# A 64-point transform folded into even and odd halves, inside a long convolution kernel

## The chip, the cores and the metric

The kernel runs on one core of a Trainium2 chip. The metric is the device time of one execution in microseconds. Besides the five engines the text speaks of their queues: SP issues most transfers, ACT some of the first ones. PE is the matrix engine, PEld its weight loads, DVE the vector engine, ACT the scalar engine, POOL GpSimd.

## What is computed

Eight sequences of 3200 positions with 256 channels go through a filter in the frequency domain and then through a gated convolution:

```python
def _attn_ref(x, w_r, w_i, b_r, b_i):
    X = np.fft.rfft(x, axis=1)
    Yr = Xr @ w_r - Xi @ w_i + b_r
    Yi = Xr @ w_i + Xi @ w_r + b_i
    Yr = np.sign(Yr) * np.maximum(np.abs(Yr) - lam, 0.0)   # lam = 0.01
    Yi = np.sign(Yi) * np.maximum(np.abs(Yi) - lam, 0.0)
    return np.fft.irfft(Y, n=x.shape[1], axis=1)
def _moe_ref(x, w_val, conv_w, w_out):
    # gate = sigmoid of a causal 5-tap convolution over positions, per channel
    return (gate * (x @ w_val)) @ w_out
```

The output of the first is the input of the second. Everything is float32, and products that must keep that precision are done either as float32 (two instructions for each product in the trace) or as three float32r products of a high and a low part.

## The kernel before

The 3200-point transform is split as 64 x 50: a position is n2 x 64 + n1 with n1 of 64 (`N1`) and n2 of 50 (`N2`). The first stage (`p1`, and `p1_first` for batch 0) is a 50-point transform over n2: each load brings four n1 for all n2 and all channels of each of two halves of n1, products with the constant `f1` of 50x50 run in quarters of the 128x128 array (50x64 weights, 512 columns), ACT copies both banks of 512 to a tile `s`, and the tile is stored to a scratch tensor `a_dram` in DRAM. In it, frequency t (25 of them, each with a real and an imaginary row, 128 rows of n1 in all) comes first, so that it can be read back (tile `a`) with the 128 rows on the partitions.

The second stage (`s2` in `p2`) is the 64-point transform over n1 with twiddle factors folded into its constant `f2`: for each t and each half of the channels one product with 128x128 weights (the data) and 128 columns (the constant, real and imaginary part). A unit u is two t, and a batch has 13 units, the last of which holds only the 25th t. Its result in PSUM (`ps_s2`, two buffers) is copied and split: ACT copies the imaginary half (L651) and casts all to its high part (L655); DVE adds real and imaginary (L658) and forms the low part (L659); ACT and DVE do the same with the sum (L662, L663). Then `mix_sum` (L676) and `mix` (L671) multiply with the filter weights in three products instead of four, DVE seeds the accumulators with the bias (L680), ACT and DVE apply the soft threshold (L687, L689). The inverse 64-point transform `s1i` (L712) works on two units in 64x64 quarters, with its constant `g1`; ACT copies the result (L723), and it is stored to `z_dram`.

After a whole batch has been stored, `positions` reads it back and does the inverse 50-point transform (`s2i`, L771, 50-column quarters), and `gated` does the value product, the convolution (ACT for the first tap, DVE for four more, L833), the sigmoid, the gate product (L845) and the output product, eight blocks per batch.

`g1` is not loaded: in batch 0 `make_g1` transposes each unit of `f2` on PE with an identity matrix `eye` (L428), and ACT scales it into place (L430).

The order on each engine is fixed when the program is built. Every step is a piece given to `Plan.add` with a due time `at` (in units; a batch is 13, and the stages of neighbouring batches overlap by the offsets in `O`), an engine, an estimated length, what it uses and what it sets. `Plan.order` lists the pieces of each engine by simulating them: among the pieces that can begin soonest it takes the one with the lowest due time. Pieces of PE have a mode, "q" for quarters, "f" or "r" for full size; a change between them costs in that model, and `together` and `hold` favour quarters next to quarters. A PSUM or SBUF buffer is reused in a ring whose size is in `SLOTS`; four tiles of two banks are shared out as two `ps_2` pairs (first stage, s1i, s2i, value and output product) and the single-bank tags.

Batch 0 starts with its own scheme: x is loaded from two queues (SP and ACT), units are done in pairs, one half evicted by DVE and the other by ACT (L523), and stores follow on both queues. Loads of constants wait for marks such as `STORED` (all first-stage stores of batch 0 issued).

## Time and profile before

| | |
|---|---|
| three runs, us | 882.78, 884.87, 886.38 (median 884.87) |
| the profiled execution, us | 881.84 (span of its instructions 880.0) |
| granted PE clock over the span | 0.99 |
| HBM traffic in the span | read 82.04 MB, written 78.64 MB |

The costliest groups on PE and DVE, in the page's fifth part: line, engine, operation, tile written and read, shapes and count, then busy time in us and the mean of one in ns, then the idle time of the engine just before them and what ended it.

```profile
L833 DVE SCALAR_TENSOR_TENSOR acc<-y_sb,cw_sb,acc 128x400 f32<-128x400 f32 x512 | 298.9, 626 | 1.7 <-ACT acc L830 1.2
L671 PE MATMUL y_ps<-w_sb,xs 128*128 128x256 f32 x1152 | 156.9, 285 | 0.6 <-DVE y_ps L680 0.3
L600 PE MATMUL s<-f_sb,a 128*128 128x128 f32 x800 | 111.6, 282 | 4.7 <-DMA f_sb<-in_f 2.9
```

Matmuls are pipelined, so the mean of one is longer than the distance to the next. Buffer numbers are left out of names: `s` is any of the tiles s1, s2; `f_sb` and `g_sb` are the constants of the two transforms; `y_p` is the result of the inverse 50-point transform.

### The profile page before, as it was taken

How to read it: one execution, taken by the hardware profiler on the slowest of the kernel's cores; microseconds unless marked ns; L12 is line 12 of the kernel's file. 1: busy time of each engine (PE TensorE's matmuls, PEld its weight loads, DVE VectorE, ACT ScalarE, POOL GpSimd, SP SyncE). 2: the span in 40 equal slices, each digit the busy share in tenths (PEclk: the TensorE clock that was granted, in tenths of full speed). 3: DMA queues.
4: the chain of work that ended last, by engine and by line, in shares of the span. 5: the costliest groups of instructions: out<-in, count | busy, mean ns of one | idle time of the engine just before them, and what ended most of it. 6: DMA issues, size and time to landing. Idle time of an engine off the chain costs nothing.

```text
span 880.0 us, 24764 instructions
## 1 busy us (share of the span) xinstructions
PE 857.8 (97%) x10358; PEld 736.3 (84%) x10358; DVE 733.8 (83%) x1289; ACT 620.3 (70%) x1046; POOL 3.7 (0%) x11
## 2 busy tenths in 40 slices
PE   6989999999999999999999999999999999999997
PEld 2468778999888999889888998889989899998774
DVE  0345778999988988798889988888997999999896
ACT  1256667878778777787787777787777876776674
POOL 0000000000000000000000000000001000000000
PEclk8889999999999999999999999999999999999999
DMA  7788887743775467654765557654665535423622
GB/s 173 213 220 250 212 255 230 250 145 127 228 243 180 144 207 227 226 168 149 232 216 181 171 178 242 219 168 155 213 211 188 163 116 185 129 93 116 203 75 75
DMA packets 103955, 162.29 MB, mean 184 GB/s; under 512 B 9666, under 2 KB 78148, under 8 KB 103844
## 3 DMA queue, kind: packets, MB, share of 16 engines
q1 hardware_dynamic: 102756, 157.44, 56.3%
q10 hardware_dynamic: 1088, 3.28, 1.5%
q8 instruction: 81, 1.33, 0.6%
q14 instruction: 30, 0.25, 0.1%
HBM read 82.04 MB, written 78.64 MB: 183 GB/s over the span
## 4 chain that ended last, share of the span: by engine, by line
PE 87%; DVE 5%; DMA 5%; ACT 1%; issue 1%; SPq 0%; ACTq 0%
PE y_ps L671 16%; PE o_ps L803 14%; PE v_ps L803 13%; PE s L600 10%; PE z_ps L712 9%; PE k_ps L676 8%; PE y_p L771 7%; PE p L553 6%; DVE acc L833 3%; DMA x<-in_x 2%; PE v_ps L799 2%; DMA a_dram<-s 1%; DMA f_sb<-in_f 1%; PE y_ps L636 1%; PE turned L428 1%
## 5 line engine op out<-in xcount | busy, mean ns | idle before, releaser
L833 DVE SCALAR_TENSOR_TENSOR acc<-y_sb,cw_sb,acc 128x400 f32<-128x400 f32 x512 | 298.9, 626 | 1.7 <-ACT acc L830 1.2
L671 PEld LDWEIGHTS y_ps<-w_sb,xs 128*128 128x128 f32 x1152 | 143.2, 188 | 18.2 <-DVE acc L833 8.5
L671 PE MATMUL y_ps<-w_sb,xs 128*128 128x256 f32 x1152 | 156.9, 285 | 0.6 <-DVE y_ps L680 0.3
L803 PE MATMUL o_ps<-gated,wo_sb 128*128 128x400 f32 x744 | 149.5, 348 | 0.0
L803 PEld LDWEIGHTS o_ps<-gated,wo_sb 128*128 128x128 f32 x744 | 134.7, 188 | 2.5
L803 PE MATMUL v_ps<-y_hl,wv_sb 128*128 128x400 f32 x648 | 129.4, 346 | 0.0
L600 PEld LDWEIGHTS s<-f_sb,a 128*128 128x128 f32 x800 | 101.4, 194 | 18.5 <-issue 9.8
L600 PE MATMUL s<-f_sb,a 128*128 128x128 f32 x800 | 111.6, 282 | 4.7 <-DMA f_sb<-in_f 2.9
L803 PEld LDWEIGHTS v_ps<-y_hl,wv_sb 128*128 128x128 f32 x648 | 114.4, 188 | 0.4 <-ACT acc L830 0.4
L689 DVE SCALAR_TENSOR_TENSOR tp<-y_ps,tp 128x512 f32<-128x512 f32 (+1 forms) x104 | 69.1, 664 | 52.1 <-ACT tp L687 51.3
L687 ACT ACTIVATE tp<-y_ps,nlam 128x512 f32<-128x512 f32 (+1 forms) x104 | 69.7, 670 | 39.5 <-PE y_ps L671 23.2
L318 ACT CAST gated<-acc 128x800 fp32r<-128x800 f32 x62 | 53.5, 862 | 62.1 <-DVE acc L845 60.3
L712 PE MATMUL z_ps<-tp,g_sb 64*64 64x256 f32 x1536 | 92.8, 379 | 0.0
L676 PE MATMUL k_ps<-w_sb,xs 128*128 128x256 f32 x576 | 85.7, 283 | 0.2 <-DVE y_ps L680 0.2
L843 ACT ACTIVATE acc<-acc 128x400 f32<-128x400 f32 x128 | 66.9, 538 | 22.4 <-DVE acc L833 22.1
L676 PEld LDWEIGHTS k_ps<-w_sb,xs 128*128 128x128 f32 x576 | 75.4, 188 | 4.0 <-issue 1.8
L771 PEld LDWEIGHTS y_p<-g_sb,zl 50*64 50x64 f32 x4096 | 67.2, 135 | 13.4 <-issue 3.7
L712 PEld LDWEIGHTS z_ps<-tp,g_sb 64*64 64x64 f32 x1536 | 55.2, 133 | 27.3 <-issue 4.9
L830 ACT ACTIVATE acc<-y_sb,cw_sb 128x400 f32<-128x400 f32 x128 | 76.3, 630 | 1.7 <-DVE gated L320 1.6
L771 PE MATMUL y_p<-g_sb,zl 50*64 50x50 f32 x4096 | 71.5, 219 | 2.5 <-DVE acc L845 1.9
L680 DVE TENSOR_TENSOR y_ps<-k_ps,bias_sb 128x512 f32<-128x512 f32 x96 | 66.4, 692 | 1.8 <-PE k_ps L676 0.5
L659 DVE TENSOR_TENSOR xs<-s,xs 128x512 fp32r<-128x512 f32 x96 | 65.2, 680 | 1.2 <-ACT xs L655 1.1
(79 smaller groups left out, 953.4 us busy)
## 6 DMA issues: line engine op xcount, KB each, us to landing
zl<-z_dram SPq DMA_DIRECT2D x128, 200.0 KB
out<-o SPq DMA_DIRECT2D x63, 400.0 KB
a<-a_dram SPq DMA_DIRECT2D x96, 256.0 KB
z_dram<-z_t SPq DMA_DIRECT2D x48, 512.0 KB
x<-in_x SPq DMA_DIRECT2D x96, 200.0 KB
a_dram<-s SPq DMA_DIRECT2D x96, 200.0 KB
x<-in_x SPq DMA_DIRECT2D x24, 192.0 KB
a_dram<-s SPq DMA_DIRECT2D x24, 192.0 KB
```

What stands on the lines that cost most here:

```text
L600: nc.tensor.matmul(spec()[:, c, :, i, :], tl[ka][:, i, c * P:(c + 1) * P], f2_of(i), start=True, stop=True)
L671: nc.tensor.matmul(p[:, 1 - r, :], xm(hx, c, r), w_sb[:, m, hw, c, :], start=False, stop=k == 5, skip_group_check=True)
L676: nc.tensor.matmul(p, sm(hx, c), w_sb[:, 0, hw, c, :], start=k == 0, stop=k == 5)
L680: nc.vector.tensor_tensor(out=buffer(ky, "ps_y", [P, 2, D]), in0=tl[kk].rearrange("p (a d) -> p a d", a=1).to_broadcast([P, 2, D]), in1=bi ...
L687: nc.scalar.activation(out=buffer(kt, "tp", [P, 2, D])[:, 0:n], in_=tl[ky][:, 0:n], func=AF.Relu, bias=nlam)
L689: add(at + 0.2, "DVE", dve(n * D), lambda: nc.vector.scalar_tensor_tensor(out=tl[kt][:, 0:n], in0=tl[ky][:, 0:n], scalar=LAM, in1=tl[kt][: ...
L712: nc.tensor.matmul(p[e * HP:(e + 1) * HP, i, j * D:(j + 1) * D], g[i * HP:(i + 1) * HP, r, e * HP:(e + 1) * HP], tl[kts[j]][i * HP:(i + 1) ...
L771: nc.tensor.matmul(pv[h][e * HP:(e + 1) * HP, c, m, :], zt[half(h), m, c * P + e * HP:c * P + (e + 1) * HP], g2_sb[half(h), :], start=True ...
L803: nc.tensor.matmul(p[:, e, 0:TB], w[:, hw, c, e * P:(e + 1) * P], src(hy, c), start=n == 0, stop=n == 5)
L830: nc.scalar.mul(block(acc(c)), y_at(k, c, 0), cw_sb[:, c, 0:1])
L833: nc.vector.scalar_tensor_tensor(out=block(acc(c)), in0=y_at(k, c, j), scalar=cw_sb[:, c, j:j + 1], in1=block(acc(c)), op0=ALU.mult, op1=A ...
L843: add(at + O["conv"] + 0.15, "ACT", act(TB, "sigmoid"), lambda c=c: nc.scalar.activation(out=acc(c), in_=acc(c), func=AF.Sigmoid), (), [kg ...
```

## The change

The 64 rows n1 of the second stage are folded: with j and -j (mod 64) taken together, a 64-point transform needs the sums for its cosine part and the differences for its sine part, 32 rows each and two special ones (0 and 32). Instead of 128 rows (real and imaginary of 64) by 128 columns there are two independent products for sum and difference rows, each 64 rows by 64 columns.

In the first stage the second half of a load is now rows -1, -2, ..., read in reverse order as the moving operand (`back`), with a constant of its own (`f1[1]`, conjugated and shifted) so that its result stands opposite to that of row j. Eviction forms sum and difference:

```diff
         def keep():
-            st = room(ks, "s1", 1024).rearrange("p (h n) -> p h n", h=NH)
-            nc.scalar.copy(out=st, in_=tl[kp])
+            room(ks, s_tag, 1024)
+            nc.scalar.copy(out=st()[:, 1], in_=tl[kp][:, 1])
...
+        def fold(h):
+            for lo, hi, n in ((0, P, slice(D, 2 * D)), (HP, P, slice(0, D))) if u == 0 else ((0, P, slice(0, 2 * D)),):
+                nc.vector.tensor_tensor(out=st()[lo:hi, h, n], in0=tl[kp][lo:hi, 0, n], in1=st()[lo:hi, 1, n], op=(ALU.add, ALU.subtract)[h])
...
+        add(at + 0.01, "ACT", act(512) + (act(D) if u == 0 else 0), keep, [kp + (0,)], [ks + (0,)] + ([START[1]] if end else []), {ks: s_tag})
+        busy = 2 * dve(D) if u == 0 else dve(512)
+        add(at + 0.01, "DVE", busy, lambda: fold(0), [kp + (0,), ks + (0,)], [ks + (1,)])
+        add(at + 0.011, "DVE", busy, lambda: fold(1), [kp + (0,)], [ks + (0,)] + ([START[0]] if end else []))
```

Rows 0 and 32 have no partner; u = 0 holds them, keeps them unfolded with smaller instructions and stores them with DMAs of their own. `a_dram` is ordered by half (sum, difference) first. Batch 0 uses the same `p1` for one u at a time; `p1_first` is gone, and each of its u is stored by four DMAs per queue.

The second stage works on four t (d), 6 d and a last t per batch, in quarters:

```diff
-    def p2(b, u, at):
...
-            for c in range(2):
-                nc.tensor.matmul(spec()[:, c, :, i, :], tl[ka][:, i, c * P:(c + 1) * P], f2_of(i), start=True, stop=True)
...
+    def p2(b, d, at):
...
+            for t in (2 * i, 2 * i + 1):
+                for c in range(2):
+                    for h in range(NH):
+                        for e in range(2):
+                            rows = slice(h * HP, (h + 1) * HP)
+                            nc.tensor.matmul(p[e * HP:(e + 1) * HP, h, c, t, :], tl[ka][rows, t, c * P + e * HP:c * P + (e + 1) * HP],
+                                             f2_sb[rows, (4 * d + t) * N1:(4 * d + t + 1) * N1], start=True, stop=True)
+        for i in range(1 if last else 2):
+            add(at + O["s2"], "PE", 450 if last else 480, lambda i=i: s2(i), [ka + (0,), ("f2", part_of(d), 0)], [k2 + (i,)],
+                {k2: "ps_s2"} if i == 0 else None, mode="f" if last else "q")
```

Half 0 gives the real part and half 1 the imaginary part, in two banks; `ps_s2` is one tile of two banks in place of two of one bank. Evictions (the copy, the cast, the sum, the two low parts) are done once for a d, each on twice the elements of before; `mixed` then does `mix_sum`, `mix` and the threshold for each of the two units as before, and `s1i` follows once per d. The last t keeps its full-size products.

```diff
-SLOTS = {"x": 3, "zl": 3, "y_hl": 2, "s1": 2, "a": 3, "xs": 2, "sx": 2, "xz": 1, "tp": 3, "zst": 2,
-         "acc": 2, "g_hl": 2, "o": 2, "ps_s2": 2, "ps_y": 1, "ps_k": 1, "ps_2": 2, "a_dram": 2, "z_dram": 2}
+SLOTS = {"x": 3, "zl": 3, "y_hl": 2, "s1": 2, "a": 2, "xs": 2, "sx": 1, "xz": 1, "tp": 3, "zst": 2,
+         "acc": 2, "g_hl": 2, "o": 2, "ps_s2": 1, "ps_y": 1, "ps_k": 1, "ps_2": 2, "a_dram": 2, "z_dram": 2}
...
-    def make_g1(at, u):
...
-                nc.tensor.matmul(p[:, r * P:(r + 1) * P], f2_sb[:, (2 * u + r) * P:(2 * u + r + 1) * P], eye_sb, start=True, stop=True)
...
+    def load_g1(at, d):
+        t = slice(d * 4 * P, NT * P if d == ND - 1 else (d + 1) * 4 * P)
+        add(at, "SP", 400, lambda: nc.sync.dma_start(out=g1_sb[:, t], in_=g1[:, t]), STORED, [("g1", d, 0)], kb=(t.stop - t.start) / 2)
```

`f2` shrinks to 1664 columns, and as it is no longer the transpose of `g1`, `g1` is loaded whole (3200 columns) in six DMAs during batch 0; `eye` is gone. The offsets in `O` have other values; one of them, `late_val`, goes from 6.023 to 7.023, which moves one block of the second-to-last batch from products with the summed late weights back to the split ones.

More of the change, by code (lines that the diff above doesn't have):

```diff
@@ new lines, in products @@
+            for k in range(2):
+                dst = p[k * HP:(k + 1) * HP, 1, :]
+                if u == 0 and k == 0:
+                    for j in range(2):
+                        nc.tensor.matmul(dst[:, j * D:(j + 1) * D], f1_sb[half(1), (1 - j) * HP:(2 - j) * HP], back[:, j, :], start=True, stop=True)
+                else:
+                    nc.tensor.matmul(dst, f1_sb[half(1), 0:HP], back[:, 2 * k:2 * k + 2, :], start=True, stop=True)
+        add(at, "PE", 890, products, [kx + (0,), kx + (1,), ("f1", 0, 0)], [kp + (0,)] + ([("turn", "p1", u)] if early else []), {kp: p_tag}, mode="q")
@@ L614, in high @@
[L614 to L617 removed]
+                room(kx, "xs", 12 * N1, F32R)
+                nc.scalar.copy(out=xs()[:, :, 0, N1:], in_=flat())
+            add(at2, "ACT", act(2 * P), high, done, [kx + (0,)], {kx: "xs"})
@@ new lines, in p2, with s1i @@
+        for i, u in enumerate(units):
+            mixed(b, u, at + i, last, kx, kq, (xs, None) if last else (xm, sm), i)
+        kz, ko, kd = ("z_ps", bd), ("z_t", bd), ("z_dram", b)
+        at = at + len(units) - 1
+        def s1i():
+            p = two_banks(kz)
+            if last:
+                nc.tensor.matmul(p[:, 0, 0:D], g1_sb[:, (NT - 1) * P:], tl[kts[0]][:, 0, :], start=True, stop=True)
+                return
+            for j, u in enumerate(units):
+                g = g1_sb[:, 2 * u * P:(2 * u + 2) * P].rearrange("p (r q) -> p r q", r=2)
+                for r in range(2):
+                    for i in range(2):
+                        for e in range(2):
+                            nc.tensor.matmul(p[e * HP:(e + 1) * HP, i, j * D:(j + 1) * D],
+                                             g[i * HP:(i + 1) * HP, r, e * HP:(e + 1) * HP],
+                                             tl[kts[j]][i * HP:(i + 1) * HP, r, :], start=r == 0, stop=r == 1)
@@ new lines, in p2, with mixed @@
+        add(at + O["s1i"] + 0.1, "ACT", act(nt * D), keep, [kz + (0,)], [ko + (0,)], {ko: "zst"})
+        add(at + O["s1i"] + 0.11, "SP", 400, store, [ko + (0,)], [kd + (u,) for u in units], {kd: "z_dram"} if d == 0 else None,
+            kb=128 * nt)
+    def mixed(b, u, at, last, kx, kq, views, i):
+        bu = (b, u)
+        ky, kk, kt = ("y_ps", bu), ("k_ps", bu), ("tp", bu)
+        n = 1 if last else 2
+        w = lambda *names: [("w", m_, h) for m_ in names for h in ("high", "low")]
+        HL = ((0, 0), (0, 1), (1, 0))
+        if last:
+            xs = views[0]
```

396 lines of the change are left out of this document (184 added, 212 removed).

## The prediction

> **What bounds the kernel now.** I read the page first (busy shares, then the chain that ended last), then the chain by line, then a table of busy time cut at the points where the same product group recurs, one cut per batch.
>
> ```profile
> PE 857.8 (97%) x10358; PEld 736.3 (84%) x10358; DVE 733.8 (83%) x1289; ACT 620.3 (70%) x1046; POOL 3.7 (0%) x11
> ...
> PE 87%; DVE 5%; DMA 5%; ACT 1%; issue 1%; SPq 0%; ACTq 0%
> ```
> ```profile
> core 0: us, PE busy (x) PEld busy (x) DVE busy (x) ACT busy (x) POOL busy (x), PEclk, DMA share, GB/s
> 46.75:151.00 104.25, 102.76 (x1116) 81.43 (x1120) 65.73 (x143) 64.89 (x119) 0.00 (x0) 0.98 0.81 232
> ...
> 284.28:385.58 101.30, 101.30 (x1294) 90.79 (x1290) 90.06 (x157) 77.61 (x130) 0.00 (x0) 1.00 0.61 195
> 385.58:487.19 101.61, 101.46 (x1295) 90.86 (x1290) 90.33 (x157) 77.64 (x130) 0.00 (x0) 1.00 0.60 195
> 487.19:589.14 101.95, 101.56 (x1294) 90.88 (x1290) 90.31 (x157) 77.81 (x130) 0.00 (x0) 1.00 0.60 195
> 589.14:690.39 101.25, 101.25 (x1294) 90.76 (x1290) 90.08 (x157) 77.62 (x130) 2.53 (x2) 1.00 0.59 190
> 690.39:791.00 100.61, 100.61 (x1273) 95.74 (x1264) 95.91 (x167) 74.62 (x130) 0.00 (x0) 1.00 0.42 136
> ```
>
> Columns of the second: stretch, its length, busy time of PE, PE's weight loads, DVE, ACT, POOL, clock, DMA share. In the four full batches PE has no gap; a batch takes 101.5 us (mean of the four lengths), DVE is busy 90.2 of it and idle 11.3, ACT 77.7. So each microsecond of PE work removed comes out of the time until DVE is in the way, 11 us further on. Batch 0 (first window) is PE's too, with DMA at 0.81; the seventh row holds the last batch's spectra, without first-stage products.
>
> **The second stage on PE.** Old: per unit of two t, four 128x128 products of 128 columns, eight instructions. New: per four t (d), 32 products of 64x64 weights and 64 columns, 64 instructions, four quarters side by side. The trace has no such shape; it has two neighbours, the 50-column quarters of y_p and the 256-column quarters of z_ps. Matmul durations overlap, so I use the distance from one start to the next in the timeline of PE:
>
> ```profile
> 391.88 0.86 PE L676 MATMUL k_ps<-w_sb,xs 128*128 128x256 f32 x6
> 392.58 2.35 PE L803 MATMUL o_ps<-gated,wo_sb 128*128 128x400 f32 x12
> ...
> 396.62 1.05 PE L600 MATMUL s<-f_sb,a 128*128 128x128 f32 x8
> 397.43 2.42 PE L803 MATMUL v_ps<-y_hl,wv_sb 128*128 128x400 f32 x12
> ...
> 403.96 1.05 PE L600 MATMUL s<-f_sb,a 128*128 128x128 f32 x8
> 404.95 1.15 PE L771 MATMUL y_p<-g_sb,zl 50*64 50x50 f32 x64
> 405.92 1.92 PE L712 MATMUL z_ps<-tp,g_sb 64*64 64x256 f32 x32
> 407.66 1.05 PE L553 MATMUL p<-x,f_sb 50*64 50x512 f32 x8
> ...
> 425.54 0.86 PE L676 MATMUL k_ps<-w_sb,xs 128*128 128x256 f32 x6
> 426.32 1.09 PE L553 MATMUL p<-x,f_sb 50*64 50x512 f32 x8
> ```
>
> An old unit takes 0.81 us (396.62 to 397.43), or 0.99 where quarters follow (403.96 to 404.95). Twelve units a batch are 9.7 to 11.9 us; I take 11.0. y_p: 0.97 us for 64 instructions, 15.2 ns each. z_ps: 1.74 for 32, 54.4 ns each. For 64 columns: proportional to columns from z_ps, 13.6 ns, 0.87 us per d; at y_p's rate, if small quarters are limited by something that doesn't grow with columns, 0.97; on the straight line between both, 15.2 + 14/206 x 39.2 = 17.9 ns, 1.14. I take 1.05, since y_p's rate is the nearest row and the line is an upper end. Six d: 6.3 (5.2 to 6.8). **Saved: 4.7 us per batch (2.9 to 6.7).**
>
> The Trainium skill, "TensorEngine Tiling (Array Packing)", section Instruction Overhead, gives about 60 cycles of overhead to each matmul, which speaks against cutting them small. If these 25 ns (an estimate at the 2.4 GHz of the page "TensorE: Matmul & The Clock Gate") came on top of each instruction's columns, a d would take 1.25 us and the saving would be 3.5. By that count z_ps would stand at 59.6 ns an instruction and y_p at 16.7; the rows have 54.4 and 15.2, so the trace does not bear it out in full.
>
> The stage becomes quarter-mode work. Going into quarters costs about 0.08 us (k_ps takes 0.70 before full-size work, 0.78 before quarters), and leaving them I take as the same. The old units often stood at such a border already; the new one can stand beside y_p, z_ps or p1. Three new groups of their own would cost 3 x 0.16 = 0.5. I take 0.3. So PE needs 101.5 - 4.7 + 0.3 = **97.1 us** per full batch (94.8 to 99.1).
>
> **What DVE gets.** Old first-stage eviction: one ACT copy of 1024 (L558). New: ACT copies 512, DVE forms a sum and a difference of 512 each, per u; for u = 0 four of 256 instead. Nearest DVE rows with a PSUM and an SBUF operand, and the copy:
>
> ```profile
> L659 DVE TENSOR_TENSOR xs<-s,xs 128x512 fp32r<-128x512 f32 x12 | 8.2, 679 | 0.0
> ...
> L558 ACT COPY s<-p 128x1024 f32<-128x1024 f32 x8 | 8.1, 1018 | 1.4 <-PE p L553 1.2
> ...
> L658 DVE TENSOR_TENSOR sx<-s,sx 128x256 f32<-128x256 f32 x13 | 5.5, 420 | 2.2 <-ACT xs L655 1.6 <-PE s L600 0.4 <-ACT sx L651 0.2
> L663 DVE TENSOR_TENSOR xs<-sx,xs 128x256 fp32r<-128x256 f32 x12 | 5.0, 417 | 0.4 <-ACT xs L662 0.4
> ```
> ```profile
> 722.04 0.68 DVE L659 TENSOR_TENSOR xs<-s,xs 128x512 fp32r<-128x512 f32 x1
> 722.64 0.41 DVE L663 TENSOR_TENSOR xs<-sx,xs 128x256 fp32r<-128x256 f32 x1
> 722.97 0.63 DVE L833 SCALAR_TENSOR_TENSOR acc<-y_sb,cw_sb,acc 128x400 f32<-128x400 f32 x1
> ```
>
> In a packed queue 512 elements take 0.60 from start to start and 256 take 0.33; the 0.68 of the group row includes a tail that the next instruction covers. Folds: 14 x 0.60 + 4 x 0.33 = 9.7 us a batch. Against that, L658, L659 and L663 now run once per d on twice the elements. From 0.33 and 0.60, an instruction costs 0.06 besides its elements; 18 fewer save 1.1. DVE's busy time becomes 90.2 + 9.7 - 1.1 = **98.8 us**, above PE's 97.1. About 2 us of it are uncovered tails that go when the queue is packed, so DVE's floor is near 96.8. ACT falls: 8 copies lose 512 elements each, about 0.43, and its own three halves merge too; near 71 of 97, no bound.
>
> So the bound moves from PE to PE and DVE together. A DVE that waits for ACT's copy with the first fold holds up everything behind it in its queue: the convolution taps, the gate product that frees v_ps, the seeds that mix waits for. Also a p1 pair of banks (two such pairs, shared with z_ps, v_ps, o_ps and y_p) is held until the second fold, some 1.9 us after the product instead of 1.0. How close DVE can come to full shows best where both were dense:
>
> ```profile
> 150.00:200.00 50.00, 49.83 (x714) 45.38 (x714) 49.00 (x87) 41.71 (x71) 0.00 (x0) 1.00 0.60 199
> ```
>
> DVE 98% there. 98.8 / 0.98 = 100.8 is the long end of a full batch if tails stay; 97.1 is the short end. I take 99.2, near the middle, since no row decides. Six full batches (1 to 6): 6 x 2.3 = **-14 us** (-26 to -4).
>
> The last batch has no folds: 4.4 of PE go, DVE has 95.9 - 1.1 and about 1 more for one block that no longer uses the late weights. -4 (nothing if DVE keeps its 4.7 us of idle, -6 with the cheap end).
>
> **Batch 0 and the start.** The 12 transposes that make g1 from f2 disappear from PE, their copies from ACT:
>
> ```profile
> 69.39 0.61 PE L428 MATMUL turned<-eye_sb,f_sb 128*128 128x128 f32 x4
> 69.75 1.65 PE L671 MATMUL y_ps<-w_sb,xs 128*128 128x256 f32 x12
> ...
> 90.09 0.71 PE L428 MATMUL turned<-eye_sb,f_sb 128*128 128x128 f32 x4
> 90.56 1.65 PE L671 MATMUL y_ps<-w_sb,xs 128*128 128x256 f32 x12
> ```
> ```profile
> 39.02 1.41 SPq L584 DMA_DIRECT2D a<-a_dram  x3
> ...
> 46.75 2.04 PE L600 MATMUL s<-f_sb,a 128*128 128x128 f32 x8 [2.91 <-DMA f_sb<-in_f]
> ```
>
> At 0.36 to 0.47 each, 12 are 5.0. With 4.4 of the second stage PE loses 9.4. The wait of 2.91 for f2 may go as well, since the first f2 load now covers a whole d, but evictions are late next there. In return g1 is loaded: 1.54 MB more, while f2 shrinks by 0.79 MB and eye's 0.07 MB go: 0.7 MB net, 3 us at 232 GB/s. DMA was busy 0.81 x 104.25 = 84 us; 84 + 3 in 95 us is 0.92, so transfers for batch 1 and g1 begin to set the pace. I take **-6** (-12 to 0).
>
> Before the first second-stage product the path is loading x, products, eviction, stores, reading back (issued 39.02). Stores of batch 0 go from 32 DMAs to 66 on two queues, the same bytes. Short issues there:
>
> ```profile
> 32.95 0.65 ACTq L489 DMA_DIRECT2D a_dram<-s  x2
> ```
>
> 34 more at 0.33 are 11 us, 5.6 per queue; the queues were mostly waiting for transfers, which hides it. If that cover is gone it is +6. The longer eviction adds some 0.7 once. I take **+1** (-1 to +6). The tail after the last batch's spectra is convolution and gating, unchanged: 0.
>
> **Sum**, against the profiled execution (881.84, span 880.0): +1 - 6 - 14 - 4 = -23, 859. The median shown, 884.87, lies 3 above that execution; I put the new median 2 above its sum: **861 us**.
>
> **Rivals.**
> (1) PE stays the bound: DVE packs into 97.1. Six batches give 26 instead of 14: 849. For it: DVE's floor of 96.8 and its 11 us of idle. Against: two engines full at once leave nothing for any wait.
> (2) DVE alone binds at about 100.8: six batches give 4: 871. For it: busy 98.8 and the 98% row. This is the rule of the same page of the Trainium skill, section PSUM Bottleneck: tiling speeds products up, not their eviction, and the copy may become the bound; the 98.8 against 97.1 agrees.
> (3) Slower: the folds are waited for in DVE's queue, and its idle time does not shrink. It decides where idle per full batch passes 101.5 - 98.8 + 9/6 = 4.2 us (9 is what the other stages give). At half the present idle, 5.6, a batch takes 104.4, six lose 17, minus 9: 892. Against: in the dense window above idle was 1 in 50.
> (4) The change doesn't do what it says: quarters of 64 columns run no faster than the old units. Then a batch stays at 101.5, the start and the transposes remain, about 877 to 884. Against: y_p and z_ps run four wide.
>
> **Chances.** Forecast (855 to 866) 0.50; (1) 0.15; (2) 0.17; (3) 0.10; (4) 0.08. The range from 846 to 880 takes in the forecast, (1) and (2), 0.82. A measurement tells about 0.5% (4.4 us) from no change: faster 0.82 (forecast, (1), (2)); same 0.10 ((4) most of all, and the mild end of (3)); slower 0.08.
>
> **What would show it.** Second stage: 64 instructions in about 1.05 us; over 1.5 refutes the step. Full batches: a cut at 99.2, PE with 2 us of idle ended by DVE, DVE busy over 97%. PE without gaps means (1); DVE at 98% with PE idle over 3 us means (2); DVE idle over 4.2 behind ACT's copy means (3). Batch 0: DMA share near 0.9. Start: the first read back of a_dram at 39 to 41 us. It goes wrong most easily in the packing of DVE, where one microsecond per batch is six in all.

## The result, and the profile after

The changed kernel takes **914.96 us** (median of four, 912.52 to 918.30) against 884.02 before (four, 882.78 to 886.38): a ratio of 1.035, interval 1.031 to 1.039. It is slower, where 861 was predicted. The profiled execution has a span of 912.2 us and a granted clock of 0.97 (880.0 and 0.99 before). One execution each of e8 and e23 below fell in a slower state; their medians and ranges leave it out.

First the page of the changed kernel, busy time of each engine and the chain that ended last, by engine:

```profile
PE 843.4 (92%) x12634; PEld 713.5 (78%) x12634; DVE 798.9 (88%) x1286; ACT 584.3 (64%) x903; POOL 4.5 (0%) x11
...
PE 56%; DVE 20%; DMA 13%; ACT 5%; issue 4%; SPq 2%; ACTq 0%; DVEq 0%
```

PE did get less to do (843.4 for 857.8), and yet it is idle for 69 us, where it was for 22. The chain, 87% PE before, now runs over PE, DVE, transfers and "issue".

Next, both kernels cut at the same place in each batch, the product of the last t in the inverse 64-point transform (L704 before, L673 after), from the table of busy time by stretch:

| batch | 0 | 1 | 2 | 3 | 4 | 5 | 6 | 7 | tail |
|---|---|---|---|---|---|---|---|---|---|
| before, us | 128.29 | 87.38 | 100.56 | 101.30 | 101.60 | 101.95 | 100.39 | 87.00 | 71.53 |
| after, us | 131.54 | 97.80 | 103.87 | 106.40 | 100.78 | 105.35 | 107.17 | 87.08 | 72.21 |

Batches 0 and 1 lose 13.7 together, batches 2 to 6 lose 17.8, the rest 0.8. The rows of the changed kernel, columns as in the prediction:

```profile
131.54:229.34 97.80, 90.65 (x1522) 79.12 (x1521) 91.35 (x147) 67.91 (x104) 0.00 (x0) 0.97 0.63 189
229.34:333.21 103.87, 98.65 (x1582) 86.97 (x1581) 99.30 (x160) 72.51 (x112) 0.00 (x0) 1.00 0.62 192
333.21:439.61 106.40, 100.50 (x1580) 88.44 (x1580) 98.19 (x157) 72.85 (x113) 0.00 (x0) 0.98 0.60 187
439.61:540.39 100.78, 97.98 (x1580) 86.64 (x1580) 98.04 (x157) 72.80 (x113) 0.00 (x0) 1.00 0.63 197
540.39:645.74 105.35, 98.54 (x1580) 86.79 (x1580) 98.12 (x157) 72.81 (x113) 0.00 (x0) 1.00 0.61 189
645.74:752.91 107.17, 101.68 (x1581) 90.56 (x1581) 99.13 (x157) 72.95 (x113) 3.38 (x2) 0.97 0.56 174
```

DVE is busy 98 to 99 us, as predicted. PE needs 98.0 in a batch without a disturbance (the fourth row). But the lengths are 101 to 107, not 99: neither engine is the bound, PE stands still for 3 to 7 us in each and DVE for 3 to 8. Adding up PE's waits in these five batches by what ended them gives 25.5 us: 10.1 in five standstills that end by "issue" (the engine waited for nothing that the profile shows), 8.1 for v_ps and 6.7 for k_ps, all but 1.7 of these behind DVE. Before, the same five batches had 0.5 in all. One such standstill, in the timeline of PE, and three rows of the table of stretches around it:

```profile
361.06 0.78 PE L787 MATMUL y_p<-g_sb,zl 50*64 50x50 f32 x35
364.60 2.66 PE L787 MATMUL y_p<-g_sb,zl 50*64 50x50 f32 x91 [2.75 <-issue]
```
```profile
358.00:361.80 3.80, 3.80 (x115) 3.41 (x115) 3.79 (x7) 2.21 (x3) 0.00 (x0) 1.00 0.64 217
361.80:364.60 2.80, 0.05 (x3) 0.00 (x1) 1.70 (x3) 0.06 (x1) 0.00 (x0) 1.00 0.66 246
364.60:368.00 3.40, 3.40 (x127) 3.40 (x127) 0.56 (x1) 2.27 (x4) 0.00 (x0) 0.51 0.50 171
```

In the middle of a group of y_p PE stops for 2.75 us, and then works at half clock for 3.4, so that the stop costs some 4.5 in all. The queue that brings instructions says what it may wait for. Its row in the page before, then after (packets, MB):

```profile
q8 instruction: 81, 1.33, 0.6%
```
```profile
q8 instruction: 99, 1.62, 0.8%
```

A packet is 16 KB; PE has 20716 instructions before and 25268 after (products and weight loads), which at 256 a packet are 80.9 and 98.7 packets. So this queue feeds PE, 256 instructions at a time. In the packet records of the trace no two of these loads begin less than 3.38 us apart, and each takes 1.1 on average, while groups of y_p and of the new second stage use 256 instructions in about 2 us. At four of the five standstills, and at one more in batch 7, a load begins within 0.7 us of the stop, though loads begin 8.7 apart on average.

The end of a stop tells more: PE goes on 1.3 to 1.5 us after a load has ended, at all five and at the one in batch 7 (the stop shown ends at 364.60, a load at 363.14). In the traces of all runs, 81 of the 82 stops of over 0.9 us by "issue" after the first 60 us end 1.1 to 1.7 us after the end of such a load. The Trainium skill, "Runtime: NRT & Kernel Launch", section Instruction fetch mechanics, has the same blocks of 16 KiB and 256 instructions on a queue of the sequencer's own, and holds that fetching is hidden, as instructions go out more slowly than they come in. The packets agree; for quarters of 50 and 64 columns the trace does not agree that it is hidden.

### The profile page after: what moved, and what is told of

Read it like the earlier page. It is cut to its first block, busy times and chain, and to the rows that moved or that the text cites. A ratio compares the mean times of both kernels' runs of the same rounds, so it can differ in the third digit from the quotient of the medians.

```text
span 912.2 us, 29342 instructions
## 1 busy us (share of the span) xinstructions
PE 843.4 (92%) x12634; PEld 713.5 (78%) x12634; DVE 798.9 (88%) x1286; ACT 584.3 (64%) x903; POOL 4.5 (0%) x11
## 4 chain that ended last, share of the span: by engine, by line
PE 56%; DVE 20%; DMA 13%; ACT 5%; issue 4%; SPq 2%; ACTq 0%; DVEq 0%
PE y_ps L729 10%; PE v_ps L819 10%; PE o_ps L819 10%; PE z_ps L681 7%; DVE acc L849 6%; PE k_ps L734 5%; PE y_p L787 5%; DMA a_dram<-s 5%; DMA x<-in_x 3%; DVE s L551 3%; PE s L610 3%; DMA zl<-z_dram 2%; PE p L532 2%; DVE y_ps L738 2%; DVE acc L861 2%
## 5 line engine op out<-in xcount | busy, mean ns | idle before, releaser
L729 PE MATMUL y_ps<-w_sb,xs 128*128 128x256 f32 x1152 | 159.3, 289 | 3.7 <-DVE st_cw L374 2.9
L729 PEld LDWEIGHTS y_ps<-w_sb,xs 128*128 128x128 f32 x1152 | 149.1, 196 | 7.8 <-issue 5.4
L819 PE MATMUL v_ps<-y_hl,wv_sb 128*128 128x400 f32 x660 | 133.1, 348 | 9.4 <-DVE s L551 7.3
L819 PEld LDWEIGHTS v_ps<-y_hl,wv_sb 128*128 128x128 f32 x660 | 117.2, 189 | 12.4 <-ACT tp L745 4.8
L551 DVE TENSOR_TENSOR s<-p,s 128x512 f32<-128x512 f32 (+2 forms) x144 | 89.6, 627 | 30.8 <-ACT s L545 16.9
L734 PE MATMUL k_ps<-w_sb,xs 128*128 128x256 f32 x576 | 92.9, 298 | 15.7 <-DVE y_ps L738 13.3
L681 PE MATMUL z_ps<-tp,g_sb 64*64 64x256 f32 x1536 | 95.0, 380 | 3.0 <-issue 1.7
L610 PEld LDWEIGHTS s<-f_sb,a 64*64 64x64 f32 x3072 | 59.2, 139 | 26.9 <-issue 17.1
L532 PE MATMUL p<-x,f_sb 50*64 50x512 f32 x256 | 73.1, 662 | 3.4 <-DMA x<-in_x 2.3
L794 ACT COPY y_sb<-y_p 128x800 f32<-128x800 f32 x64 | 52.9, 827 | 32.2 <-PE y_p L787 32.0
```

The lines of the kernel that those rows point to most:

```text
L532: nc.tensor.matmul(p[k * HP:(k + 1) * HP, 0, :], f1_sb[half(0), 0:HP], xt[half(0), k * 512:(k + 1) * 512], start=True, stop=True)
L551: nc.vector.tensor_tensor(out=st()[lo:hi, h, n], in0=tl[kp][lo:hi, 0, n], in1=st()[lo:hi, 1, n], op=(ALU.add, ALU.subtract)[h])
L610: nc.tensor.matmul(p[e * HP:(e + 1) * HP, h, c, t, :], tl[ka][rows, t, c * P + e * HP:c * P + (e + 1) * HP], f2_sb[rows, (4 * d + t) * N1: ...
L681: nc.tensor.matmul(p[e * HP:(e + 1) * HP, i, j * D:(j + 1) * D], g[i * HP:(i + 1) * HP, r, e * HP:(e + 1) * HP], tl[kts[j]][i * HP:(i + 1) ...
L729: nc.tensor.matmul(p[:, 1 - r, :], xm(hx, c, r, i), w_sb[:, m, hw, c, :], start=False, stop=k == 5, skip_group_check=True)
L734: nc.tensor.matmul(p, sm(hx, c, i), w_sb[:, 0, hw, c, :], start=k == 0, stop=k == 5)
```

## The experiments

Five theories stood at first: **A**, the folds' work on DVE binds; **B**, the second stage with one pair of banks and one `sx` makes chains; **C**, the bank pair of the first stage is held until the second fold; **D**, ACT waits for stores of u = 0 to free an `s1` buffer; **F**, PE's instruction supply. "Order kept" means that every engine has the same order of work as in the changed kernel.

| run | median, us | ratio to before | batches 0, 1 | batches 2 to 6 |
|---|---|---|---|---|
| before | 884 | | 215.7 | 505.8 |
| after | 914.96 | 1.035 (1.031 to 1.039) | 229.3 | 523.6 |
| e1_tiny_folds | 913.29 | 1.032 (1.026 to 1.038) | 224.4 | 522.3 |
| e2_early_release | 923.03 | 1.043 (1.036 to 1.050) | 229.1 | 532.6 |
| e3_before_plus | 909.83 | 1.030 (1.024 to 1.035) | 235.0 | 520.4 |
| e4_pool_folds | 962.66 | 1.088 (1.082 to 1.094) | 236.7 | 564.3 |
| e5_s1_three | 911.45 | 1.029 (1.024 to 1.035) | 228.4 | 524.3 |
| e6_s2_wide | 904.64 | 1.022 (1.017 to 1.027) | 228.6 | 521.0 |
| e7_before_narrow | 900.56 | 1.018 (1.012 to 1.024) | 224.7 | 518.0 |
| e8_spread_back | 928.22 | 1.043 (1.033 to 1.053) | 242.9 | 526.4 |
| e9_g1_loaded | 885.06 | 1.001 (0.998 to 1.005) | 222.8 | 506.8 |
| e10_whole_stores | 906.78 | 1.023 (1.019 to 1.027) | 223.6 | 522.6 |
| e11_tiny_wide | 901.54 | 1.017 (1.009 to 1.025) | 224.8 | 518.2 |
| e12_tiny_planned | 910.08 | 1.027 (1.023 to 1.032) | 230.0 | 514.0 |
| e13_no_wait | 910.98 | 1.031 (1.027 to 1.035) | 226.6 | 527.4 |
| e16_no_wait_wide | 904.82 | 1.023 (1.019 to 1.026) | 224.6 | 523.0 |
| e20_three_more | 893.95 | 1.010 (1.006 to 1.015) | 224.1 | 507.8 |
| e21_whole_three | 905.00 | 1.025 (1.020 to 1.029) | 224.9 | 519.7 |
| e22_short_chain | 887.50 | 1.004 (1.000 to 1.007) | 225.3 | 506.2 |
| e23_all | 885.66 | 1.000 (0.997 to 1.004) | 221.1 | 502.0 |

The last two columns are of one profiled execution each, in which a standstill more or less is 2 to 5 us; the medians decide. B has no run of its own. In the five batches of the changed kernel PE waits 0.6 us in all before products of the second stage (for a transfer; one standstill left out), so the pair of banks is not what holds them; in batch 0 it holds the second d for 3.5 us (a row under "The start"). Whether the one `sx` costs something was not tried.

### A: the folds' work

Order kept, ACT copies both banks, DVE folds two columns only:

```diff
-            nc.scalar.copy(out=st()[:, 1], in_=tl[kp][:, 1])
+            nc.scalar.copy(out=st(), in_=tl[kp])
...
+                n = slice(n.start, n.start + 2)
                 nc.vector.tensor_tensor(out=st()[lo:hi, h, n], ...
```

> The changed kernel with its order of instructions unchanged; ACT copies all 1024 elements of a first-stage result, and each of DVE's folds works on 2 columns in place of 256 or 512, so sums and differences are left out and the output is not the reference's. Theory A (DVE has become the bound: the folds' 9.7 us per batch leave it no slack, and every wait on it is now PE's): full batches fall from a mean of 104.7 us to 97-99, the time to 865-880. Theory B (the quarter-mode second stage does it, with one ps_s2 and one sx buffer in place of two and its longer chain of evictions): the time stays above 900. Theory C (bank pairs held until the second fold) expects the same as A.

Measured 913.3. One of its rows, batch 4, shows DVE with 7.3 us less than in the row of the changed kernel above, and a length that did not follow:

```profile
435.62:537.88 102.26, 98.50 (x1580) 86.66 (x1581) 90.73 (x157) 75.87 (x112) 0.00 (x0) 1.00 0.63 195
```

So the folds' work alone is not what the changed kernel waits for. The other way round, the kernel before with that much DVE work added in batches 1 to 7 (ACT copies one bank, DVE copies the whole of the other twice, the order made anew):

```diff
-            nc.scalar.copy(out=st, in_=tl[kp])
+            nc.scalar.copy(out=st[:, 1], in_=tl[kp][:, 1])
...
+            nc.vector.tensor_copy(out=st[:, 0], in_=tl[kp][:, 0])
```

> The kernel before with the folds' work alone added to DVE in batches 1 to 7: ACT copies one bank of a first-stage result, DVE copies the other twice. The second stage stays at full size. Theory A: DVE goes from 90.2 to 99.9 us per batch against PE's 101.5, both full, so batches become 103-106 and the time 895-915. Theory B: 884-889, the added work fits beside PE.

Measured 909.8, 25 us more: 14.6 in batches 2 to 6, DVE busy 97.1 to 99.5 of 103.3 to 104.8, and 24 in batch 1. In the trace 8.2 of the 14.6 are waits of PE that the kernel before does not have, 3.4 of them by "issue". So this much DVE work, together with the order that goes with it, costs when PE still needs 101; as the order is a new one, how much of the 25 is the work's is not shown.

The folds on POOL, which the profile shows idle (batches 1 to 7, ACT copies both banks to a buffer, POOL folds from there, order made anew):

```diff
+                    nc.gpsimd.tensor_tensor(out=st()[lo:hi, h, n], in0=rv[lo:hi, 0, n], in1=rv[lo:hi, 1, n], ...
```

> The changed kernel with the folds of batches 1 to 7 on POOL: ACT copies all 1024 elements to SBUF, POOL forms sum and difference from there to a second tile (one 512-column tensor_tensor of POOL took 1.29 us before, so 20.6 us per batch on an idle engine). Theory A: DVE falls to 89 us per batch, full batches to 97-99, time 865-885. If POOL's reads of SBUF hold up DVE's, DVE's instructions get longer and the time stays above 895. Theory B: above 900.

Measured 962.7. The groups of this run, the convolution taps on DVE and the folds on POOL:

```profile
L868 DVE SCALAR_TENSOR_TENSOR acc<-y_sb,cw_sb,acc 128x400 f32<-128x400 f32 x512 | 349.0, 727 | 3.6 <-ACT acc L865 2.8
L565 POOL TENSOR_TENSOR s<-s 128x512 f32<-128x512 f32 (+1 forms) x126 | 166.3, 1338 | 597.9 <-ACT s L550 540.7 <-DMA zl<-z_dram 37.2 <-ACT xs L674 11.4
```

The same 512 taps take 727 ns in the mean where they take 626 in the kernel before: 50 us more for DVE (349.0 for 298.9), of the 68 (seven batches of 9.7) that moving the folds should have freed. The mean hides two kinds: the 432 taps that no fold on POOL overlaps take 629 ns, the 70 that lie beside one for more than half of their time take 1348 (the other ten lie between).

### C, D and an order: held banks, the store, the offsets

ACT copies both banks, so that they are free before the folds, and DVE folds inside SBUF (order kept):

```diff
-            nc.scalar.copy(out=st()[:, 1], in_=tl[kp][:, 1])
+            nc.scalar.copy(out=st(), in_=tl[kp])
...
+                    nc.vector.tensor_tensor(out=st()[lo:hi, 0, n], in0=st()[lo:hi, 0, n], in1=st()[lo:hi, 1, n], op=ALU.add)
```

> The changed kernel with its order of instructions unchanged; ACT copies all 1024 elements, and DVE folds within SBUF (sum, then sum minus twice the second), with as much DVE work as before the edit. The bank pair is free after ACT's copy. Theory A (DVE's work binds): 905-920, since the work is the same. Theory C (the bank pair held until the second fold stalls PE, 1.6 us and a drop of the clock per batch): 890-900.

Measured 923.0, above both ranges; C alone falls. PE's waits for v_ps in the five batches are gone (8.1 us before the edit), but those for k_ps grew from 6.7 to 20.5. Three `s1` buffers, order kept:

```diff
-bufs=SLOTS[tag])
+bufs=3 if tag == "s1" else SLOTS[tag])
```

> The changed kernel, order unchanged, with three buffers in place of two for the first-stage tile that is stored to a_dram. Theory D (at each batch turn ACT waits 2 to 3 us for such a buffer, since the stores of u = 0 hold SP with many small DMAs, and the threshold, the bank pairs and PE wait behind ACT): that wait goes, 2 to 4 us per batch, the time falls by 12 to 25 to 890-903. Theory F (PE runs out of instructions): no more than 4 us.

Measured 911.5: ACT's wait for stores fell from 29.6 us to 14.9 (in the five batches from 7.9 to 0.2), PE's waits did not (25.5 to 26.4). D alone falls too. Two offsets of the order as they were before:

```diff
-O = {'spread': -0.013,
+O = {'spread': 0.139,
...
-     'later': 4.433,
+     'later': 4.822,
```

> The changed kernel with two of the planner's offsets as they were (spread 0.139 and later 4.822 in place of -0.013 and 4.433), which place DVE's conversion of the late matrices in batch 0. If conversions in one block on DVE hold up the seeds there (PE gaps of 2.1 and 2.9 us before 120 us, each followed by half clock): batches 0 and 1 together are 5 to 12 us shorter, the time 903-910. If not: within 4 us of the changed kernel.

Measured 928.2 (918.3 to 928.7), where 903 to 910 was expected if they were the cause: setting them back does not help. A new order alone moved the median by 13 us, though the intervals of the two ratios overlap, so runs with the order kept weigh more than others.

### F: the instruction supply

Half as many second-stage products, each on 128 columns (order kept; columns of two t with the data of one):

```diff
-            for t in (2 * i, 2 * i + 1):
+            for t in (2 * i,):
...
-f2_sb[rows, (4 * d + t) * N1:(4 * d + t + 1) * N1]
+f2_sb[rows, (4 * d + t) * N1:(4 * d + t + 2) * N1]
```

> The changed kernel, order of steps unchanged, with half as many second-stage products on twice the columns: one product of 128 columns in place of two of 64, so every second t is computed from its neighbour's data and the output is not the reference's. The columns streamed are the same, the instructions of a d go from 128 (loads and products) to 64. Theory F (small quarter products use up PE's instructions faster than the next 256 arrive; PE stands still with no wait on an engine and the clock falls after it): those standstills go from the full batches, the time falls by 8 to 20, to 895-907. Theory D: the same as the changed kernel within 4 us.

Measured 904.6, 10 us less than the changed kernel for the same number of columns, and three standstills in the five batches instead of five (6.0 us for 10.1). Then the kernel before, its DVE, ACT and order untouched, only with the first stage's products of batches 2 to 7 cut into eight of 64 columns:

```diff
+            w = 64 if b > 1 else 512
+            for lo in range(0, 512, w):
...
+                        nc.tensor.matmul(p[k * HP:(k + 1) * HP, h, lo:lo + w], f1_sb[half(h), :], ...
```

> The kernel before with the first-stage products of batches 2 to 7 cut into eight of 64 columns each: the same columns streamed, 128 instructions per u where there were 16. Theory F: PE gets standstills without a wait on an engine, granted clock under 1.00 in some full batches, batches 103-106, the time 895-910. If small products cost only their own time at 15.2 ns an instruction (1.0 us per u for 0.93): within 6 us of before, 884-891.

Measured 900.6: **17 us from narrow products alone.** The worst stop, in the timeline of PE, and the stretches of it and after it:

```profile
343.62 2.08 PE L773 MATMUL y_p<-g_sb,zl 50*64 50x50 f32 x128
348.60 2.08 PE L602 MATMUL s<-f_sb,a 128*128 128x128 f32 x8 [2.90 <-issue]
```
```profile
345.70:348.60 2.90, 0.00 (x0) 0.00 (x1) 1.90 (x5) 1.68 (x2) 0.00 (x0) 0.86 0.67 250
348.60:352.00 3.40, 3.40 (x13) 3.39 (x14) 0.39 (x2) 1.28 (x4) 0.00 (x0) 0.50 0.53 189
```

Two groups of y_p in a row, 256 instructions in 2.08 us, then nothing for 2.90, then half clock for 3.4: what the changed kernel shows, in a kernel that has nothing else of the change. The time of the narrow products themselves is the small part: batch 4, in which PE never stops, takes 102.1 for 101.6. What else its trace shows is 8.8 us of standstills by "issue" in the whole kernel (1.1 before) and about 5 lost at half clock after them. F is shown as a part of the cause. It isn't all: the wide run still stands 21 above before.

### The start

The last stores of the first stage decide when the second may begin. SP's queue in the timeline and the first second-stage product, before and then after, with ACT's issues and copies after:

```profile
24.34 11.23 SPq L489 DMA_DIRECT2D a_dram<-s  x12
...
41.77 2.08 PE L600 MATMUL s<-f_sb,a 128*128 128x128 f32 x8 [0.45 <-DMA a<-a_dram]
```
```profile
25.52 16.96 SPq L493 DMA_DIRECT2D a_dram<-s  x24
...
23.60 5.25 ACTq L493 DMA_DIRECT2D a_dram<-s  x8
28.89 1.07 ACT L545 COPY s<-p 128x512 f32<-128x512 f32 x2 [5.58 <-DMA a_dram<-s]
...
47.48 0.33 PE L610 MATMUL s<-f_sb,a 64*64 64x64 f32 x4 [1.64 <-DMA a<-a_dram]
...
53.38 1.98 PE L610 MATMUL s<-f_sb,a 64*64 64x64 f32 x64 [3.50 <-DVE xs L659]
```

Twice the stores occupy SP for 5.7 us longer, ACT's copies wait behind ACT's own issues (5.25 us for the eight that end just before 28.89), and the first second-stage product comes at 47.5 instead of 41.8. Stores not cut by rows, order kept:

```diff
-st()[k * HP:k * HP + N2, hs, n:], rows)
+st()[k * HP:k * HP + N2, hs, n:], ((0, N2),) if early else rows)
```

> Changed kernel, order unchanged; the stores of batch 0's first stage aren't cut by rows, so they take half as many DMAs. If the start (first second-stage product at 47.45 against 41.77) is late because of the number of issues on the two queues, of which ACT's stand between its evictions, that product comes at 42 to 44 and the whole is 910 to 912. If transfers set it, it stays at 47 or gets later, as fewer and larger transfers spread worse, and the whole is 915 or more.

Measured 906.8, 8 us less; SP's twelve take 10.25, the first product comes at 44.4. So the number of issues is 3.1 of the start's 5.7; the other 2.6 stay open, and so does why the whole gains more than the start does (batch 0 is 6.2 shorter in the trace).

The other part of batch 0 alone, `g1` loaded in the kernel before instead of made by transposes (its columns lie by t, so that the inverse products take some constants from other places):

```diff
-                nc.tensor.matmul(p[:, r * P:(r + 1) * P], f2_sb[...], eye_sb, start=True, stop=True)
+            add(at, "SP", 400, lambda: nc.sync.dma_start(out=g1_sb[:, s], in_=g1[:, s]), STORED, ...
```

> One part of the change alone, on the kernel before: the constant g1 is loaded in six DMAs during batch 0 instead of being made by twelve transposes, and the identity matrix goes. The prediction's step for the transposes (5.0 us of PE, 3 us more of DMA) gives -2 to -5: 879 to 882. If DMA sets the pace of batch 0 already, it stays within 2 us of 884. If the load of g1 is what cost the changed kernel its start or its batch 1 (+10.4), batch 0 or batch 1 gets longer here and the whole is at 888 or more.

Measured 885.1, no change: the 5 us of PE are not gained. In the profiled execution, the longest of the ten (891.5), batch 0 to its marker is 10 shorter, and batch 1 17 longer.

### Two at once

Folds on two columns with wide products; the same folds with the order made anew (in the planner 60 ns each); folds that wait for nothing (ACT copies both banks, and DVE clears two columns of a tile of its own in place of each fold); and that with wide products:

```diff
-                nc.vector.tensor_tensor(out=st()[lo:hi, h, n], in0=tl[kp][lo:hi, 0, n], in1=st()[lo:hi, 1, n], ...
+                nc.vector.memset(idle_sb, 0.0)
```

> Changed kernel, order unchanged; folds on 2 columns (ACT copies both banks) and half as many second-stage products on twice the columns; the output is not the reference's. Alone the first gave 913 and the second 905. If the folds' work is covered and only the instruction supply of PE costs, it is 903 to 907. If each of the two hides behind the other (PE's standstills behind DVE's waits), both gone give 885 to 897, below what they give one by one. If the order alone costs the rest, it stays at 903 or above.

> Changed kernel with folds on 2 columns and the order made anew for that (ACT copies both banks, the folds told to the planner as 60 ns); the output is not the reference's. If the order fits only the work it was made for, so that folds' time is paid as waits of PE whether or not they run, full batches come down to 98 to 101 and the whole to 880 to 895. If PE's own standstills are what is left (theory of instruction supply), it stays at 900 to 912, with issue standstills of 1.5 to 3 us in the full batches. Any other order alone moved the time by about 10 us, so the standstills are to be looked at, not the sum alone.

> Changed kernel, order unchanged; ACT copies both banks, and in place of each fold DVE clears 2 columns of a tile of its own, which waits for nothing; the output is not the reference's. With folds on 2 columns that still wait for ACT's copy it was 913, and in its five full batches PE waited about 14 us for DVE (k_ps 9.5, v_ps 4.2). If those waits come from the folds' wait for ACT in DVE's in-order queue (the mechanism of the prediction's third rival), they go, and the time is 893 to 903. If they come from the second stage's single buffer and its chain over ACT and DVE, or from the order, they stay, and the time is 908 to 916.

> The same with half as many second-stage products on twice the columns, so that the folds' work, their wait and half of the added instructions are gone (with the wait kept it was 901.5); the output is not the reference's. If the wait in DVE's queue and the instruction supply are the two causes in the full batches, these fall below 100 and the whole to 880 to 893, with the start's 6 us still in it. If the second stage's chain is the cause, it stays at 896 to 905.

Measured 901.5, 910.1, 911.0 and 904.8. The first lies between the range for two that hide each other (885 to 897) and that for supply alone (903 to 907), 3 below wide products alone, which is not clear of noise; the order made anew gains nothing in the sum (e12, with standstills of 2.7 in it), and the wait of the folds for ACT, **the mechanism that the prediction's third rival named, falls as a cause by itself**: without it PE waits as long (25.1 us in five batches), now at k_ps (13.9 for 6.7) and no longer at v_ps (0.2 for 8.1). The turn of a batch, where the first stage of a new one begins, shows why. In the changed kernel (timeline, PE, ACT and DVE):

```profile
348.29 4.45 DVE L849 SCALAR_TENSOR_TENSOR acc<-y_sb,cw_sb,acc 128x400 f32<-128x400 f32 x8
...
351.51 1.56 PE L729 MATMUL y_ps<-w_sb,xs 128*128 128x256 f32 x12
352.17 0.59 ACT L545 COPY s<-p 128x512 f32<-128x512 f32 x1 [3.00 <-DMA a_dram<-s]
...
352.79 0.69 DVE L551 TENSOR_TENSOR s<-p,s 128x512 f32<-128x512 f32 x1
...
354.75 0.68 ACT L745 ACTIVATE tp<-y_ps,nlam 128x512 f32<-128x512 f32 x1
354.82 1.51 PE L819 MATMUL v_ps<-y_hl,wv_sb 128*128 128x400 f32 x7 [1.75 <-DVE s L551]
```

With three `s1` buffers:

```profile
346.80 4.45 DVE L849 SCALAR_TENSOR_TENSOR acc<-y_sb,cw_sb,acc 128x400 f32<-128x400 f32 x8
...
347.53 0.59 ACT L545 COPY s<-p 128x512 f32<-128x512 f32 x1
...
351.17 0.68 DVE L551 TENSOR_TENSOR s<-p,s 128x512 f32<-128x512 f32 x1
...
353.19 2.40 PE L819 MATMUL v_ps<-y_hl,wv_sb 128*128 128x400 f32 x12 [1.66 <-DVE s L551]
```

And with folds that wait for nothing, two buffers:

```profile
349.07 1.59 PE L728 MATMUL y_ps<-w_sb,xs 128*128 128x256 f32 x12
349.68 1.01 ACT L546 COPY s<-p 128x1024 f32<-128x1024 f32 x1 [2.95 <-DMA a_dram<-s]
...
352.83 0.70 ACT L744 ACTIVATE tp<-y_ps,nlam 128x512 f32<-128x512 f32 x1
...
355.13 0.94 PE L733 MATMUL k_ps<-w_sb,xs 128*128 128x256 f32 x6 [1.94 <-DVE idle_sb L550]
```

In the first, ACT waits 3.00 us for a store before it may copy the first-stage pair (until 352.76), and DVE is at eight taps until 352.74: the fold, and with it the banks that v_ps needs, wait behind both, which end at the same moment. In the second ACT copies at once (347.53), but the fold stands behind eight taps in DVE's queue until 351.17: v_ps waits 1.66 all the same. In the third no fold is in the way of v_ps, but ACT waits 2.95 for the store again, and behind that copy and what follows it in ACT's queue stands the threshold of y_ps, ready since 350.7 and begun at 352.83, which the next seed and k_ps wait for. Two things cover each other, and a chain runs through both.

### Both covers and the chain

No folds, wide products and three buffers; the same with a threshold formed on DVE alone, without ACT's step; and that with whole stores (all in the changed kernel's order):

```diff
+bufs=3 if tag == "s1" else SLOTS[tag])
...
-            nc.scalar.activation(out=buffer(kt, "tp", [P, 2, D])[:, 0:n], in_=tl[ky][:, 0:n], func=AF.Relu, bias=nlam)
+            buffer(kt, "tp", [P, 2, D])
...
+            nc.vector.tensor_scalar(out=tl[kt][:, 0:n], in0=tl[ky][:, 0:n], scalar1=LAM, scalar2=0.0, ...
```

> Changed kernel, order unchanged, four things gone at once: the folds' work and their wait (DVE clears 2 columns instead), half of the second-stage products (the other half on twice the columns), and the wait of ACT for stores (three s1 buffers instead of two); the output is not the reference's. Without the third buffer it was 904.8, and PE waited 1.8 to 2.4 us for k_ps once a batch where the stage of a new batch begins and 0.8 once more. If the wait there has two covers (folds behind taps in DVE's queue, ACT behind a store), of which taking away either one alone moved nothing, it goes now: 885 to 897. If the chain from one mix to the next (threshold on ACT and DVE, seed, k_ps) sets it whatever stands in front, it stays at 900 to 906.

> As the one before, and the threshold without its step on ACT (DVE alone forms it from y_ps), so that the chain from one mix to the next is shorter by ACT's 0.7 us and by what stands ahead of it in ACT's queue; the output is not the reference's. If this chain sets the waits that are left in the full batches (k_ps 15.1 us in five of them) and in batch 0, they shrink by half or more and the whole falls by 8 to 20 below the run before. If not, it is within 3 us of it.

> As the run with the shortened chain (887.5), and the stores of batch 0 not cut by rows, as in the run that took 8 us off the changed kernel; the output is not the reference's. If the start's part is separate from the others, it comes off again: 878 to 883. If batch 0 is held by the second stage's single buffer whatever the start, the time gained there is lost before batch 1: 885 to 889. Either way batches 2 to 6 stay at 99 to 100 where PE has no standstill.

Measured **894.0**, **887.5** and **885.7**. The third buffer, worth 3.5 with folds (915.0 to 911.5, intervals overlapping) and 1.8 beside whole stores (e21, below), is worth 10.9 once the folds are gone and the products wide; the folds are worth nothing without it (904.6 with them and 904.8 without, products wide). So at least these two have to go together; folds, wide products and three buffers at once were not run. At the turn k_ps now waits 0.63 us. The shorter chain takes off 6.5 more (less than the 8 to 20 expected, and the two ratios' intervals overlap by a little). In the traces PE's waits for k_ps in the five batches fall from 9.7 us to 2.8 (the 15.1 in the expectation is the figure of the run without the third buffer): the chain from one mix over threshold, seed and k_ps to the next was what set most of them. The two profiled executions are equally long (889.6 and 889.2), as standstills by "issue" rose from 4.0 to 8.1 there. Batches 3 and 4 of the run with the short chain:

```profile
330.19:429.32 99.13, 98.06 (x1388) 86.08 (x1388) 89.17 (x157) 68.38 (x99) 0.00 (x0) 1.00 0.64 200
429.32:532.06 102.74, 99.80 (x1389) 87.89 (x1389) 89.23 (x157) 68.70 (x99) 0.00 (x0) 0.98 0.64 193
```

Without a standstill a batch takes 99.1 and PE is idle for 1.1 of it; the second row has a stop of 2.32 us and half clock after it. In the last run the first second-stage product comes at 43.5 instead of 47.4 and batch 0 is 4 shorter, as expected of the start, but the median says 1.8 less, with runs from 878 to 888: whether the start adds in full can't be told.

Last, the two cures that leave the kernel whole, stores not cut and three buffers:

> Changed kernel, order unchanged, complete: stores of batch 0 not cut by rows (alone 906.8) and three s1 buffers (alone 911.5). If both add up it is 902 to 905. If the third buffer gives only what its wait was worth at the start, it stays at 906 to 908. The kernel before is not reached by either.

Measured 905.0, 10 us better than the changed kernel and 2.5% behind the one before. No version that beats the kernel before came out of these runs.

## Why the prediction was wrong

**The pieces were mostly right.** The second stage takes 1.04 us per d, start to start, predicted 1.05; here in the timeline of PE in the changed kernel:

```profile
431.00 1.11 PE L610 MATMUL s<-f_sb,a 64*64 64x64 f32 x64
432.04 0.97 PE L734 MATMUL k_ps<-w_sb,xs 128*128 128x256 f32 x6
```

 DVE is busy 98.0 to 99.3 us a full batch, predicted 98.8. PE needs 98.0, predicted 97.1 with 94.8 to 99.1 as bounds. The tail is unchanged.

**The step that failed is "I take 99.2, near the middle, since no row decides".** It put a full batch between PE's need and DVE's dense packing, as if every wait of one engine were covered by work of the other. The five batches measured took 104.7 in the mean. What stands in place of the 99.2, per batch: 98.0 of PE, 2.0 in standstills of PE's supply (10.1 in five), 3.0 in waits for v_ps and k_ps (14.8 in five), and 1.5 by which PE was busy longer than undisturbed (99.5 in the mean), some 1.0 of it in three stretches of 3.4 us at half clock; the sum is 104.5. Two mechanisms were missing:

- The prediction priced 64 instructions per d by the row of y_p and asked only how long they take. It did not ask how fast PE's instructions can come: the narrow products in the kernel before cost 17 us with the rest untouched, and PE goes on after a stop 1.1 to 1.7 us after the end of a load of instructions. The weighing of overhead per instruction looked at a cost of each instruction; the cost was one of many in a row.
- "Where a stall goes, what is late next" was asked of engines' totals, not of the single things on the path: one y_ps, one k_ps, one ACT queue in which a copy that waits for a store stands ahead of the threshold, and one DVE queue in which a fold stands behind eight taps.

**The third rival** got the side and the size (a batch at 104.4, measured 104.7; total 892, measured 915, since batch 1 and the start went wrong as well). That 104.4 is so near is luck, as 10.1 of the 25.5 us of waits have a cause that it does not name. Half of its sign came: DVE is idle for 6.2 us a batch, over the 4.2, but not behind ACT's first-stage copy: before the folds it is idle for 0.9 in all five batches together. Its mechanism, folds waited for in DVE's queue, is one of two covers: taken away alone it is worth nothing (e13), and with it gone the wait for the store is worth 10.9. It was given 0.10 because DVE stood idle for 1 us of 50 in a dense window of the kernel before. That window (150 to 200) begins 22 us after the marker of its batch; the turn, where most of the waits for v_ps begin (20 us after the marker), is outside it, so it could not stand for a whole batch.

**The first rival** (PE without gaps) and **the second** (DVE at 98% of a batch) didn't come about: DVE has 92 to 97% of a batch. **The fourth** is refuted by the 1.04.

**Batch 0 and the start.** For the start +1 was taken and +6 given "if that cover is gone". It is +5.7; whole stores bring the first product forward by 3.1 and take 8 off the kernel. The cover was not there: SP's and ACT's queues were full of issues in that stretch, and ACT's evictions stood between them. From there to the marker batch 0 gained 2.4 us (84.09 instead of 86.52), predicted 6; `g1` loaded alone gives nothing in the median, so its PE time did not come off the whole. Batch 1, forecast 2.3 shorter as one of six, is 10.4 longer: PE waits 7.1 us in it instead of 0.2 and is busy for 3.5 more, with 6.8 us at half clock. Batch 7 gained nothing, predicted 4: PE did 2.4 less there, and one standstill of 2.43 took it back.

**What stays open.** Batches 0 and 1 together still stand 5.4 behind in the run with everything taken away. The trace shows waits there for the one pair of banks of the second stage (3.5 us at the second d) and for k_ps (6.0 in both batches, 0.2 before), and once 2.9 for a conversion on DVE (`st_cw`); a second pair has no place in the plan of eight banks, and it wasn't tried. Whether the folds' work alone would cost the changed kernel something once the other causes are gone was not tried either; the kernel before with such work added, in a new order, suggests that it would.

## What to carry to other kernels

Before cutting products small, count PE's instructions in the densest few microseconds of the order as well as per batch, and look for stretches in which 256 of them pass faster than the instruction queue's loads follow each other in the trace. When a bound moves from one full engine to two nearly full ones, don't place the result between their busy times: list the buffers of which there is one and the instructions that stand ahead of each release in its engine's queue. And when undoing one suspect changes nothing, undo it together with the next one at the same place before clearing it: two waits that end at the same moment hide each other.

## What the hardware showed that was not expected

- PE stops for 0.9 to 4.3 us, mostly in or next to dense groups of narrow quarters, with nothing waited for, and goes on 1.1 to 1.7 us after a load of 256 instructions on its own queue has ended (81 of 82 stops). These loads never begin less than 3.32 us apart in the 20 traces.
- The clock falls to half for 3.4, 6.8 or (once) 10.2 us soon after some such stops, and not after others. After the first 60 us the beginnings of these stretches in the clock records lie, within each trace, whole multiples of 3.413 us apart (in the changed kernel 364.70, 706.03 and 733.34: 100 and 8 of them). With batches 1 to 7 of the 19 traces that have such stretches cut into intervals on that grid, all 55 intervals at full clock with at least 1.9 us of idle PE were followed by half clock, 21 of 69 with 1.4 to 1.9, and 2 of 2858 with less. So a stop that falls across a border of the grid (568.51 to 570.85, border 569.50) can pass without. One of 1.64 us (a wait of k_ps for DVE) was followed by half clock, as two stretches of the changed kernel show. The Trainium skill, "TensorE: Matmul & The Clock Gate", section Why this matters for your kernels, puts the limit at gaps of about 3 us; the trace does not agree that shorter ones are free:

```profile
703.67:705.31 1.64, 0.00 (x0) 0.03 (x1) 1.64 (x4) 1.33 (x4) 0.00 (x0) 1.00 0.93 302
706.10:709.50 3.40, 3.40 (x17) 3.39 (x16) 2.58 (x4) 1.72 (x3) 0.00 (x0) 0.51 0.52 148
```

- With folds on an idle POOL the DVE taps beside one took 1348 ns in the mean instead of 629, and the kernel, in an order made anew, was 5% slower than with the folds on DVE.
